# Reordering the opening of a fused attention and feed-forward kernel: exponentials, fillers, pieces and a split normalization

## The chip, the cores and the metric

The kernel runs on one core of one Trainium2 chip. The metric is the time of one execution in microseconds of the device (us), as a median of several runs. The profile is one such execution, recorded; it counts from the first instruction and its span is some 2 us shorter than the timed run. PE is the matrix engine, DVE the vector engine, ACT the scalar engine, POOL the GpSimd engine; "landing" is the time at which a load from memory is complete. Every engine's own stream is in a fixed order (the program is scheduled by hand), so an instruction that waits holds up all that stand behind it on its engine.

## The reference

```python
def _attn_ref(q, k, v):                      # each (8, 8, 576, 64): batch, heads, tokens, head size
    q_s = np.exp(q - q.max(-1, keepdims=True)); q_s /= q_s.sum(-1, keepdims=True) + 1e-09
    k_s = np.exp(k - k.max(2, keepdims=True));  k_s /= k_s.sum(2, keepdims=True) + 1e-09
    kv = np.einsum('bhsd,bhse->bhde', k_s, v)
    return np.einsum('bhsd,bhde->bhse', q_s, kv)

def _moe_ref(x, w1, w2, w3, w_out):          # x (4608, 512), d_ff 1024
    h = (x @ w1) * (x @ w2) @ w3
    return h @ w_out
```

The output of the attention, with heads and head size joined, is `x`. All inputs and the output are float32.

## The kernel before

The kernel folds `w3 @ w_out` into one matrix once ("W3O", eight groups `ft` of 128 rows): each W3 tile is loaded, cast to 16 bit, transposed on PE (`w3_t`), copied by DVE, and multiplied with `w_out` (eight matmuls for each group). Then, for each chunk of 512 tokens, `s1` makes (x @ w1) * (x @ w2) and `s2` multiplies by W3O. The attention of a batch is made of pieces: exponentials of q and k on ACT (`exp_q`, `exp_k`), sums and reciprocal on DVE (`sum_q`), a multiplication that normalizes q (`norm_q`), PE transposes of the result and a DVE copy of them (`piece_t`), `piece_kv`, and `piece_x`, which makes x. All of W3, w_out, the first batch and the w1 and w2 quarters are loaded through one queue, in that order; "fillers" are matmuls on zeros.

```python
    filler(16)
    w3_both(0)                      # cast on POOL and ACT, then w3_t
    wo_c(0, pcopy, acopy)
    filler(4)
    w3_part((0, 0))                 # (ft, gp): two of the eight matmuls of group ft
    # ... fillers 3, 3, 3 between groups 1 to 2 ...
    w3_part((2, 0), (2, 1), (0, 2), (1, 2), (2, 2))
    w3_both(3)
    wo_c(3, pcopy, acopy)
    w3_c(4, pcopy)
    w3_t(4)
    w3_part((3, 0), (3, 1), (3, 2))
    # ... last part of groups 0 to 3, each followed by its copy on ACT; w3_c(5 to 7), w3_t(5) ...
    w3_rest(4, pAB(), acopy)        # eight matmuls, then the copy into W3O
    w3_t(6)
    for hh in range(2):
        exp_q(0, 0, hh)
        sum_q(0, 0, hh)
    norm_q(0, 0, nc.gpsimd)
    w3_rest(5, pAB(), acopy)
    w3_t(7)
    # ... the same for q1, then exp_k(0, 0), v0 casts ...
    w3_rest(6, pAB(), acopy)
    piece_t(0, 0)
    wp7 = pO()
    w3_mm(wp7, 7, range(N_FT))
    piece_kv(0, (0,))
    piece_t(0, 1)
    # ... exp_k(0, 1), copy of W3O[7], v1 casts: the second qsT copy of piece_t is ahead of them on DVE ...
    piece_x(0, 0, acopy, acopy, apart=True)
    piece_kv(0, (1,), by_head=True)
    # ... piece_x(0, 1), then s1 of chunk 0 ...
```

The softmax here doesn't subtract the row's maximum and nothing guards it: scores larger than these inputs give would overflow.

## Time and profile before

| what | value |
|---|---|
| median of the first three runs | 240.61 us |
| span of the profiled run | 238.1 us |
| PE busy | 229.4 us (96%) |
| first s1 matmul of chunk 0 | 33.78 us |
| first s2 matmul of chunk 0 | 47.60 us |
| first s1 matmul of chunk 1 | 58.15 us |

The page of the kernel before: busy time of each engine with its share of the span and its instructions, then the chain of work that ended last, by engine.

```profile
PE 229.4 (96%) x1769; PEld 107.5 (45%) x1769; DVE 126.4 (53%) x214; ACT 101.3 (43%) x182; POOL 66.6 (28%) x61
...
PE 91%; DVE 5%; POOL 1%; ACT 1%; issue 1%; DVEq 0%; ACTq 0%; POOLq 0%
```

No load is in that chain. The waits of PE in the kernel before (engine, line and tile, who ended the wait: total us, how often, longest; the wait of 1.2 us at the very start is left out):

```profile
PE att L176 <- POOL eqn L138: 0.9, 1, 0.9
PE att L176 <- DVE eqn L138: 0.8, 1, 0.8
PE po L186 <- DVE kv_556 L164: 0.6, 1, 0.6
PE att L154 <- DVE v_0_73 L124: 0.5, 1, 0.5
PE po L329 <- DVE qsT L324: 0.3, 1, 0.3
```

All of them lie before 53 us; afterwards PE has no wait worth naming. The first, third and fourth belong to the first batch, the second to the second batch, the fifth to the W3 groups. The chain of waits of the kernel before from 22 to 32 us (start us, duration us, what) shows how the first batch hangs together:

```profile
22.44 0.59 ACT W3O_91 L372
23.03 0.59 ACT eq L119
...
23.64 1.43 DVE ds L131 x2
...
25.51 2.13 POOL eqn L138
27.64 0.05 issue
27.68 0.68 PE att L176 x9
28.36 1.73 PE po L329 x8
...
31.14 0.76 DVE qsT L178
31.90 0.40 DVE v_0_73 L124
```

Two facts stand out. The exponential of q0 runs behind a W3O copy at 22.44 us, though q0 landed at 20.25 us. And the last cast of v1, which landed at 29.07 us, runs only behind the second qsT copy.

The timeline of PE in the kernel before, around the fifth W3 transposes (start us, duration us, what; the idle time before it and who ended it stand in brackets).

```profile
15.64 0.61 PE L319 MATMUL att<-ident,w_288 128*128 128x128 f16 x8
16.14 0.62 PE L319 MATMUL att<-ident,w_304 128*128 128x128 f16 x8
17.04 0.60 PE L329 MATMUL po<-wo_83,qsT 128*128 128x512 f16 x2 [0.28 <-DVE qsT L324]
```

The trace says that the fifth transposes (w_304) were released at 16.09 us by POOL's cast of that tile; the last fillers had ended at 13.34 us.

### The profile page before, as it was taken

Reading aid. Unit: us, or ns where it says so; the run is one execution under the profiler, and the core shown is the slowest. Engines: PE = TensorE matmul, PEld = TensorE weight load, DVE = VectorE, ACT = ScalarE, POOL = GpSimd, SP = SyncE. Lnnn points to the kernel's source line nnn. Section 1 sums busy time; section 2 is a strip of 40 time slices with the busy share of each in tenths; the row PEclk is TensorE's granted clock in tenths of the full one; section 3 lists DMA queues with packets and bytes.
Section 4 is the critical chain, followed back from the end, with each engine's and each line's share of the span. In section 5 each row is a group of like instructions: output and inputs, shape, how many; then the busy total and the mean of one; then the engine's idle time right before and its main releaser. Section 6 shows DMA issues by size and latency. Waiting matters only on the chain.

```text
span 238.1 us, 4550 instructions
## 1 busy us (share of the span) xinstructions
PE 229.4 (96%) x1769; PEld 107.5 (45%) x1769; DVE 126.4 (53%) x214; ACT 101.3 (43%) x182; POOL 66.6 (28%) x61
## 2 busy tenths in 40 slices
PE   8999889989999999999999999999999999999993
PEld 2455444444444444444444444444444444444442
DVE  0232854498847745854763586477464344343432
ACT  4425953664665644643545354346441112222100
POOL 3453776080370260361045036023400000000000
PEclk9999999999999999999999999999999999999999
DMA  6999999999269999659979929932632222232244
GB/s 248 395 408 390 373 349 364 391 392 365 63 129 383 391 278 331 256 110 303 376 154 340 377 46 247 322 107 47 122 70 44 44 44 47 46 70 60 45 91 132
DMA packets 39702, 52.08 MB, mean 219 GB/s; under 512 B 16512, under 2 KB 20864, under 8 KB 39680
## 3 DMA queue, kind: packets, MB, share of 16 engines
q1 hardware_dynamic: 39280, 51.26, 69.2%
q10 hardware_dynamic: 400, 0.52, 0.8%
q8 instruction: 14, 0.23, 0.4%
q14 instruction: 8, 0.07, 0.1%
HBM read 38.80 MB, written 9.44 MB: 203 GB/s over the span
## 4 chain that ended last, share of the span: by engine, by line
PE 91%; DVE 5%; POOL 1%; ACT 1%; issue 1%; DVEq 0%; ACTq 0%; POOLq 0%
PE pab L239 52%; PE po L286 20%; PE pab L286 5%; PE att L377 3%; PE pab L329 3%; PE att L154 3%; PE att L186 2%; PE po L329 2%; DVE ds L131 1%; PE att L319 1%; POOL eqn L138 1%; DVE qsT L324 1%; PE att L176 1%; DVE eqn L138 1%; ACT eq L119 1%
## 5 line engine op out<-in xcount | busy, mean ns | idle before, releaser
L138 POOL TENSOR_TENSOR eqn<-eq,dr 128x1152 f16<-128x1152 f16 x15 | 31.7, 2116 | 89.6 <-DVE dr L136 59.5
L286 PEld LDWEIGHTS <-abT 128*128 128x128 f16 x296 | 28.4, 98 | 32.7 <-DVE abT L249 0.4
L288 DVE TENSOR_SCALAR osb<-po 128x512 f32<-128x512 f32 (+1 forms) x29 | 19.8, 683 | 22.1 <-PE po L286 19.1
L131 DVE TENSOR_REDUCE ds<-eq 128x9 f32<-128x576 f16 x32 | 23.6, 746 | 1.1 <-ACT eq L119 1.1
L119 ACT ACTIVATE eq<-st 128x576 f16<-128x576 f32 x32 | 21.2, 689 | 0.3 <-DMA st<-in_q_dram 0.3
L112 ACT ACTIVATE ek<-st 128x576 f16<-128x576 f32 x32 | 20.7, 682 | 0.0
L239 PE MATMUL pab<-xT,w_0_75 128*128 128x512 f16 x72 | 18.5, 379 | 0.0
L239 PE MATMUL pab<-xT,w_3_78 128*128 128x512 f16 x72 | 18.4, 380 | 0.0
L239 PE MATMUL pab<-xT,w_2_77 128*128 128x512 f16 x72 | 18.4, 380 | 0.0
L239 PE MATMUL pab<-xT,w_1_76 128*128 128x512 f16 x72 | 18.3, 379 | 0.0
L239 PE MATMUL pab<-xT,w_1_80 128*128 128x512 f16 x72 | 18.3, 379 | 0.0
L239 PE MATMUL pab<-xT,w_2_81 128*128 128x512 f16 x72 | 18.3, 379 | 0.0
L239 PE MATMUL pab<-xT,w_3_82 128*128 128x512 f16 x72 | 18.3, 379 | 0.0
L239 PE MATMUL pab<-xT,w_0_79 128*128 128x512 f16 x72 | 18.3, 379 | 0.0
L202 ACT CAST xT<-att 128x512 f16<-128x512 f32 x14 | 7.5, 589 | 10.6 <-PE att L186 10.6
L239 PEld LDWEIGHTS <-w_0_79 128*128 128x128 f16 x72 | 7.0, 98 | 8.8 <-issue 0.6
L286 PE MATMUL po<-W3O_87,abT 128*128 128x512 f16 (+1 forms) x29 | 10.9, 377 | 0.0
L286 PE MATMUL po<-W3O_88,abT 128*128 128x512 f16 (+1 forms) x29 | 10.9, 376 | 0.0
L286 PE MATMUL po<-W3O_89,abT 128*128 128x512 f16 (+1 forms) x29 | 10.9, 376 | 0.0
L286 PE MATMUL po<-W3O_90,abT 128*128 128x512 f16 (+1 forms) x29 | 10.9, 376 | 0.0
L286 PE MATMUL po<-W3O_91,abT 128*128 128x512 f16 (+1 forms) x29 | 10.9, 376 | 0.0
L286 PE MATMUL po<-W3O_92,abT 128*128 128x512 f16 (+1 forms) x29 | 10.9, 376 | 0.0
(315 smaller groups left out, 352.6 us busy)
## 6 DMA issues: line engine op xcount, KB each, us to landing
st<-in_q_dram SPq DMA_DIRECT2D x16, 576.0 KB, 8.7
st<-in_k_dram SPq DMA_DIRECT2D x16, 576.0 KB, 7.1
st<-in_v_dram SPq DMA_DIRECT2D x15, 576.0 KB, 7.8
out_dram<-osb SPq DMA_DIRECT2D x67, 128.0 KB, 2.6
st<-in_moe_w_dram SPq DMA_DIRECT2D x15, 512.0 KB, 9.0
st<-in_moe_w_out_dram SPq DMA_DIRECT2D x4, 512.0 KB, 7.0
st<-in_v_dram SPq DMA_DIRECT2D x2, 288.0 KB, 11.8
st<-in_moe_w_dram SPq DMA_DIRECT2D x2, 256.0 KB, 10.7
```

Of the source, the lines that this page charges most:

```text
L112: nc.scalar.activation(out=eks[(b, i)][:, :, hh, :], in_=qkv32[("k", b, i)][:, hh].rearrange("p (r d) -> p r d", r=R), func=AF.Exp)
L119: nc.scalar.activation(out=eqs[(b, i)][:, :, hh, :], in_=qkv32[("q", b, i)][:, hh].rearrange("p (r d) -> p r d", r=R), func=AF.Exp)
L131: nc.vector.tensor_reduce(out=dss[(b, i)][:, :, hh], in_=eqs[(b, i)][:, :, hh, :], axis=AX.X, op=ALU.add)
L138: eng.tensor_tensor(out=eqn.rearrange("p r h d -> p (r h) d"), in0=eqs[(b, i)].rearrange("p r h d -> p (r h) d"), in1=dr[:, :, None].broad ...
L154: nc.tensor.matmul(kvp[64 * hh:64 * hh + 64, g, 65 * i:65 * i + 65], lhsT=eks[(b, i)][rows, r, hh], rhs=v16buf[b % 2][rows, 2 * i + hh, r, ...
L186: nc.tensor.matmul(out.rearrange("p (r s) -> p r s", s=SP), lhsT=kvs[(b, i)][rows, g], rhs=qsTs[(b, i)][rows, r0:r1, 64 * g:64 * g + 64], ...
L202: copy(out=dst[:, hh], in_=xps[hh])
L239: nc.tensor.matmul(p, lhsT=wsb[qt][:, ct, fo:fo + P], rhs=xT[:, ct, t0:t0 + CH], start=(ct == 0), stop=(ct == N_CT - 1))
L286: nc.tensor.matmul(po[:, 0:n1 - n0], lhsT=abT[(j, ft)][:, tb * P:(tb + 1) * P], rhs=W3O[ft][:, n0:n1], start=(ft == 0), stop=(ft == N_FT - 1))
L288: nc.vector.tensor_scalar(out=osb[:, n0:n1], in0=po[:, 0:n1 - n0], scalar1=ISC, scalar2=None, op0=ALU.mult)
L329: nc.tensor.matmul(wps, lhsT=w3Ts[ft][:, gt, :], rhs=wosb[gt // 2][:, gt % 2, :], start=(gt == 0), stop=(gt == N_FT - 1))
L377: nc.tensor.matmul(wp[:, 0], lhsT=zero[:, 0:P], rhs=zero, start=True, stop=True)
```

## The change

The intent: put the q exponentials of the first batch ahead of the W3O copies on ACT, cut fillers from 29 matmuls to 16, put pieces of the first batch between the last W3O groups, and split each normalization of the second batch over DVE and POOL. Two things are not in the cut below: the cast of the first w1 quarter is all on POOL (a quarter of it was on ACT), and the casts of v of the second batch stand elsewhere in the order. The diff, cut to its core:

```diff
-    filler(16)
+    filler(8)
     w3_both(0)
     wo_c(0, pcopy, acopy)
-    filler(4)
+    filler(2)
     # ... three more filler(3) become filler(2) ...
-    w3_part((2, 0), (2, 1), (0, 2), (1, 2), (2, 2))
+    w3_part((2, 0), (2, 1), (0, 2))
     w3_both(3)
+    w3_part((1, 2), (2, 2))
     wo_c(3, pcopy, acopy)
-    w3_c(4, pcopy)
+    w3_c(4, pcopy, acopy)
+    w3_part((3, 0), (3, 1), (3, 2))
     w3_t(4)
-    w3_part((3, 0), (3, 1), (3, 2))
     # ...
-    w3_rest(4, pAB(), acopy)
+    w3_mm(wps[4], 4, range(N_FT))
     w3_t(6)
+    for i in range(2):
+        for hh in range(2):
+            exp_q(0, i, hh)
+            sum_q(0, i, hh)
+        norm_q(0, i, nc.gpsimd)
+        if i == 0:
+            acopy(out=W3O[4], in_=wps[4])
+            w3_mm(wps[5], 5, range(N_FT))
+            w3_t(7)
     # ... exp_k(0, 0), v0 casts, copy of W3O[5] ...
+    w3_mm(wps[6], 6, range(N_FT))
+    w3_mm(wps[7], 7, range(4))
     piece_t(0, 0)
-    wp7 = pO()
-    w3_mm(wp7, 7, range(N_FT))
-    piece_kv(0, (0,))
-    piece_t(0, 1)
+    w3_mm(wps[7], 7, range(4, N_FT))
     # ... exp_k(0, 1), copies of W3O[6], W3O[7] ...
+    piece_kv(0, (0,))
     # ... v1 casts, now ahead of the second qsT copy ...
+    piece_t(0, 1)
-    piece_x(0, 0, acopy, acopy, apart=True)
+    piece_x(0, 0, acopy, acopy, apart=(pAB, pAB))
     # ... second batch:
-    norm_q(1, 0, nc.gpsimd)        # within s1 of the last pair
-    norm_q(1, 1, nc.vector)
+    norm_q(1, 0, nc.vector, nc.gpsimd)   # behind that pair; rows 0:5 on DVE, 5:9 on POOL
+    norm_q(1, 1, nc.vector, nc.gpsimd)
-    s2(0, 0, alt=True)
+    s2(0, 0, alt=True, on_act=True)      # result scaled and copied by ACT, also for s2(0, 1)
     piece_t(1, 0)
-    piece_t(1, 1)
     s2(0, 2, alt=True)
+    piece_t(1, 1)
```

More of the change, by code (lines that the diff above doesn't have):

```diff
@@ L132, in sum_q, with norm_q @@
                                 axis=AX.X, op=ALU.add)
-    def norm_q(b, i, eng):
-        dr = drs[(b, i)].rearrange("p r h -> p (r h)")
-        nc.vector.reciprocal(out=dr, in_=dss[(b, i)].rearrange("p r h -> p (r h)"))
+    def norm_q(b, i, *engs):
+        dr = drs[(b, i)]
+        nc.vector.reciprocal(out=dr.rearrange("p r h -> p (r h)"),
+                             in_=dss[(b, i)].rearrange("p r h -> p (r h)"))
         eqn = attn.tile([P, R, 2, D], F16, tag="eqn", name="eqn", bufs=4)
-        eng.tensor_tensor(
-            out=eqn.rearrange("p r h d -> p (r h) d"),
-            in0=eqs[(b, i)].rearrange("p r h d -> p (r h) d"),
-            in1=dr[:, :, None].broadcast_to([P, 2 * R, D]), op=ALU.mult)
+        cuts = (0, R) if len(engs) == 1 else (0, 5, R)
+        for eng, r0, r1 in zip(engs, cuts, cuts[1:]):
+            eng.tensor_tensor(
+                out=eqn[:, r0:r1].rearrange("p r h d -> p (r h) d"),
+                in0=eqs[(b, i)][:, r0:r1].rearrange("p r h d -> p (r h) d"),
+                in1=dr[:, r0:r1].rearrange("p r h -> p (r h)")[:, :, None].broadcast_to(
+                    [P, 2 * (r1 - r0), D]), op=ALU.mult)
         eqns[(b, i)] = eqn
@@ L188, in x_mm, with piece_x @@
                          start=True, stop=True)
-    def piece_x(b, i, *copies, apart=False):
+    def piece_x(b, i, *copies, apart=()):
         if apart:
-            xps = [pO(), pAB()]
+            xps = [p() for p in apart]
         else:
@@ L277, with s2 @@
     outv = out.rearrange("(b s r) c -> b r s c", r=R, s=SP)
-    def s2(j, tb, alt=False, cuts=(0, C), mid=None):
+    def s2(j, tb, alt=False, cuts=(0, C), mid=None, on_act=False):
         osb = ffn.tile([P, C], F32, tag="osb", name="osb", bufs=4)
@@ L287, in s2 @@
                                  rhs=W3O[ft][:, n0:n1], start=(ft == 0), stop=(ft == N_FT - 1))
-            nc.vector.tensor_scalar(out=osb[:, n0:n1], in0=po[:, 0:n1 - n0], scalar1=ISC,
-                                    scalar2=None, op0=ALU.mult)
+            if on_act:
+                nc.scalar.mul(out=osb[:, n0:n1], in_=po[:, 0:n1 - n0], mul=ISC)
+            else:
+                nc.vector.tensor_scalar(out=osb[:, n0:n1], in0=po[:, 0:n1 - n0], scalar1=ISC,
+                                        scalar2=None, op0=ALU.mult)
             for h in range(2):
@@ L368, in w3_part @@
             w3_mm(wps[ft], ft, (2 * gp, 2 * gp + 1))
-    def w3_rest(ft, wp, copy):
-        w3_mm(wp, ft, range(N_FT))
-        copy(out=W3O[ft], in_=wp)
     def filler(n):
@@ L377, in filler @@
             nc.tensor.matmul(wp[:, 0], lhsT=zero[:, 0:P], rhs=zero, start=True, stop=True)
-    filler(16)
+    filler(8)
     w3_both(0)
     wo_c(0, pcopy, acopy)
-    filler(4)
+    filler(2)
     w3_part((0, 0))
-    filler(3)
+    filler(2)
     w3_both(1)
     wo_c(1, pcopy, acopy)
-    filler(3)
+    filler(2)
     w3_part((1, 0), (0, 1), (1, 1))
@@ L390 @@
     wo_c(2, pcopy, acopy)
-    filler(3)
-    w3_part((2, 0), (2, 1), (0, 2), (1, 2), (2, 2))
+    filler(2)
+    w3_part((2, 0), (2, 1), (0, 2))
     w3_both(3)
+    w3_part((1, 2), (2, 2))
     wo_c(3, pcopy, acopy)
-    w3_c(4, pcopy)
+    w3_c(4, pcopy, acopy)
+    w3_part((3, 0), (3, 1), (3, 2))
     w3_t(4)
-    w3_part((3, 0), (3, 1), (3, 2))
     for ft in range(4):
@@ L404 @@
     w3_c(7, pcopy)
-    w3_rest(4, pAB(), acopy)
+    wps += [pAB(), pAB(), pAB(), pO()]
+    w3_mm(wps[4], 4, range(N_FT))
     w3_t(6)
-    for hh in range(2):
-        exp_q(0, 0, hh)
-        sum_q(0, 0, hh)
-    norm_q(0, 0, nc.gpsimd)
-    w3_rest(5, pAB(), acopy)
-    w3_t(7)
-    for hh in range(2):
-        exp_q(0, 1, hh)
-        sum_q(0, 1, hh)
-    norm_q(0, 1, nc.gpsimd)
+    for i in range(2):
[7 more added lines that the diff above has]
+            w3_t(7)
     exp_k(0, 0, 0)
@@ L421 @@
     cast_v(0, 0, acopy, slice(1, 2))
-    w3_rest(6, pAB(), acopy)
+    acopy(out=W3O[5], in_=wps[5])
+    w3_mm(wps[6], 6, range(N_FT))
+    w3_mm(wps[7], 7, range(4))
     piece_t(0, 0)
-    wp7 = pO()
-    w3_mm(wp7, 7, range(N_FT))
-    piece_kv(0, (0,))
-    piece_t(0, 1)
+    w3_mm(wps[7], 7, range(4, N_FT))
     exp_k(0, 1, 0)
     exp_k(0, 1, 1)
-    acopy(out=W3O[7], in_=wp7)
+    acopy(out=W3O[6], in_=wps[6])
+    acopy(out=W3O[7], in_=wps[7])
+    piece_kv(0, (0,))
     cast_v(0, 1, pcopy, slice(0, 1))
@@ L433 @@
     cast_v(0, 1, pcopy, slice(1, 2), slice(5, 9))
-    piece_x(0, 0, acopy, acopy, apart=True)
+    piece_t(0, 1)
+    piece_x(0, 0, acopy, acopy, apart=(pAB, pAB))
     piece_kv(0, (1,), by_head=True)
-    cast_w(0, 0, acopy, slice(0, 2), slice(0, P))
-    cast_w(0, 0, pcopy, slice(0, 2), slice(P, 2 * P))
-    cast_w(0, 0, pcopy, slice(2, 4), slice(0, P))
-    cast_w(0, 0, pcopy, slice(2, 4), slice(P, 2 * P))
+    for cts in (slice(0, 2), slice(2, 4)):
+        for f in range(2):
+            cast_w(0, 0, pcopy, cts, slice(f * P, f * P + P))
     x8 = pAtt([P, 2, 512], F32)
     x8_mm(0, [x8[:, 0], x8[:, 1]], (0,))
-    piece_x(0, 1, acopy, vcopy, apart=True)
+    piece_x(0, 1, acopy, vcopy, apart=(pAB, pO))
     x8_mm(0, [x8[:, 0], x8[:, 1]], (1,))
@@ L459 @@
     sum_q(1, 0, 0)
-    def second_q():
-        exp_q(1, 0, 1)
-        sum_q(1, 0, 1)
-        norm_q(1, 0, nc.gpsimd)
-    s1_pair(0, (6, 7), second_q, lambda: (exp_q(1, 1, 0), exp_q(1, 1, 1)))
+    s1_pair(0, (6, 7), lambda: exp_q(1, 0, 1), lambda: (exp_q(1, 1, 0), exp_q(1, 1, 1)))
+    sum_q(1, 0, 1)
+    norm_q(1, 0, nc.vector, nc.gpsimd)
     sum_q(1, 1, 0)
     sum_q(1, 1, 1)
-    norm_q(1, 1, nc.vector)
+    cast_v(1, 0, pcopy)
+    norm_q(1, 1, nc.vector, nc.gpsimd)
     exp_k(1, 0, 0)
     exp_k(1, 0, 1)
-    cast_v(1, 0, pcopy)
-    s2(0, 0, alt=True)
+    s2(0, 0, alt=True, on_act=True)
     exp_k(1, 1, 0)
     exp_k(1, 1, 1)
-    s2(0, 1)
-    piece_t(1, 0)
-    piece_t(1, 1)
     cast_v(1, 1, pcopy, slice(0, 1))
     cast_v(1, 1, acopy, slice(1, 2))
+    s2(0, 1, on_act=True)
+    piece_t(1, 0)
     pc = pieces(1)
     s2(0, 2, alt=True)
+    piece_t(1, 1)
     pc[0]()
```

## The prediction

> What bounds it now. The page gives a span of 238.1 us, PE busy 229.4 us (96%); the chain of waits is 91% PE. From 58.2 us, where chunk 1 starts, the timeline of PE shows no gap worth naming, so the change can pay only in its first 58 us. There the page's DMA row is at 9 tenths: load landings are fixed by the queue (last W3 tile 18.75, q0 20.25, q1 23.02, last half of v1 29.07, w2 first quarter 32.07, last half batch-1 v 50.20 us).
>
> Three losses in that stretch. (1) By the timelines, the first-batch q exps wait for the W3O_91 copy (22.44), itself behind PE, although q0 landed at 20.25; sum, reciprocal and POOL normalization (2.12 us) follow, and the first-batch transposes wait 0.93 us on PE (27.68). (2) The last v1 cast, landed 29.07, sits on DVE behind the second qsT copy, runs at 31.82; PE then waits 0.55 us, and 0.56 us for kv. s1 starts at 33.78. (3) Second-batch transposes wait 0.83 us for DVE's eqn (52.62).
>
> What the change does. It removes 13 fillers (8 initial, 5 at 216 ns each): PE reaches the fourth W3 transposes when its cast is ready (about 13.1, was 15.64), so W3O groups end 2 us earlier. q exps start at about 20.3, POOL's first eqn is ready near 24.9 (was 27.63). The v1 cast runs at once (29.1); first-batch kv, x follow the landing: s1 starts at about 31.4, gain 2.3 us. It cannot start much earlier: w2's first quarter is cast by 32.7 and needed 1.73 us after s1's start. Later quarters are cast at 34.67 to 42.23, each 0.2 to 1.5 us before need.
>
> Second batch: landings again bound it. The split costs less than it seems: the Trainium skill (SBUF — State Buffer, section "Who interferes with whom") says a DVE instruction with two SBUF inputs excludes a GpSimd instruction that reads SBUF. This trace agrees: POOL's v cast took 1.80 us beside DVE's eqn, 0.66 elsewhere. So the halves run one after the other, estimated 0.7 + 0.95 us, hardly better than one engine. I estimate eqn(1,0) at 48.8, eqn(1,1) at 51.5, last v cast 52.2, kv about 52.3 (was 54.95), chunk 1's s1 at 55.5 (was 58.15). Moving two evictions to ACT (0.6 us each) costs nothing there.
>
> Sum: 2.3 us from the first batch, about 0.3 more from the second: 2.6 us, all kept by the PE-bound rest. Predicted 238.0 us, range 236.8 to 239.6. Chances: faster by over 2% 0.03, within 0.94, slower 0.03.
>
> What would show it. Timelines: first filler ends about 4.8, w_3 transposes at 13.1; first eqn ends about 24.9; first s1 matmul 31.0 to 31.9; chunk-0 s2 about 45.3; POOL's eqn half stretched beyond 0.95 us or DVE's beyond 0.7; chunk 1's s1 near 55.5; from there every later instruction shifted by the same 2.6 us. Landing times unchanged to 0.3 us.
>
> What would make it wrong. The fillers keep the clock: the Trainium skill (TensorE: Matmul & The Clock Gate, section "What's actually happening") has half rate until a busy window of some 3.4 us; in this trace full clock begins 5.8 us in, and the removed 8 leave gaps under 1 us, so I expect it to stay. If not, PE falls behind the loads and up to 2 us go. Second: w1/w2 quarters landing late, with POOL casts just in time, could stall s1. Third: the eqn halves colliding with POOL's v cast longer than I assume, which would take the second-batch 0.3 us and more. On the other side, if q1 lands earlier and both batches run at landing times, the gain is 3.5 us.

## The result, and the profile after

The changed kernel took 237.94 us (median of 4 runs, 237.59 to 238.45), the kernel before 240.75 us (median of 4, 240.04 to 241.52). The ratio is 0.9884, with a 95% interval of 0.9849 to 0.992: a gain of 1.2%.

The page of the changed kernel, same parts:

```profile
PE 227.0 (96%) x1756; PEld 106.3 (45%) x1756; DVE 125.6 (53%) x213; ACT 102.8 (44%) x184; POOL 66.9 (28%) x63
...
PE 76%; DMA 18%; SPq 2%; POOL 1%; ACT 1%; issue 0%; DVE 0%
```

PE lost 2.4 us of busy time, the 13 fillers, and the span fell by 2.3 us. That looks like a full explanation; the experiments show that it is a coincidence. The second line seems to be a better clue: loads (DMA) now hold 18% of the chain. Between 24 and 53 us the chain of waits of the changed kernel reads:

```profile
17.31 10.98 DMA st<-in_v_dram
28.29 8.96 DMA st<-in_moe_w_dram
...
37.30 0.94 POOL w L93
38.24 11.03 DMA st<-in_k_dram
...
49.29 1.27 ACT ek L112 x2
...
50.58 1.63 POOL eqn L141
...
52.25 0.40 PE att L180 x4
```

This clue fails, though. The loads are on the path to a k load of the second batch, not on that to the start of s1, and they enter the chain only by the step from ACT's exponential of k (until 50.56 us) to POOL's half of a normalization (from 50.58 us). The program has no such dependency: that exponential stands behind the normalization, which does not read its result. In the run with the old fillers (below) the same exponential ended at 50.31 us and the same multiplication began only at 50.81. In both profiles it begins as POOL's cast of v ahead of it ends (50.62 and 50.85 us). The view infers its links from the times of semaphores, and here it took a coincidence for a cause. Whether loads bind has to be read from the timelines and tested.

The timeline of PE in the changed kernel, from the first batch's transposes to s1:

```profile
26.52 0.68 PE L180 MATMUL att<-ident,eqn 128*128 128x128 f16 x9
27.03 1.03 PE L336 MATMUL po<-wo,eqn 128*128 128x512 f16 x4
27.99 0.48 PE L158 MATMUL att<-v,ek 64*64 64x65 f16 x36
28.71 0.68 PE L180 MATMUL att<-ident,eqn 128*128 128x128 f16 x9 [0.24 <-DVE rc L166]
...
30.97 0.22 PE L190 MATMUL att<-qsT,kv 64*64 64x64 f16 x4 [0.19 <-DVE qsT L182]
31.37 0.40 PE L190 MATMUL pab<-qsT,kv 64*64 64x512 f16 x1 [0.18 <-DVE kv L168]
```

and DVE's in the same stretch, which answers to the end of the chain shown of before:

```profile
29.76 0.49 DVE L124 CAST v<-st 128x320 f16<-128x320 f32 x1 [0.73 <-DMA st<-in_v_dram]
30.16 0.75 DVE L182 COPY qsT<-att 128x1152 f16<-128x1152 f16 x1
```

The v1 cast stood idle for its load and ran 0.02 us after the landing at 29.74 us; in the kernel before it ran 2.75 us after the landing (31.82 against 29.07). The three waits of the first batch, 2.0 us together, became three of 0.2 us each.

| landmark, us | before | after | predicted |
|---|---|---|---|
| last half of v1 landed | 29.07 | 29.74 | unchanged |
| first s1 matmul of chunk 0 | 33.78 | 31.74 | 31.4 |
| first s2 matmul of chunk 0 | 47.60 | 45.78 | 45.3 |
| second-batch kv | 54.95 | 52.58 | 52.3 |
| first s1 matmul of chunk 1 | 58.15 | 55.88 | 55.5 |

The loads landed 0.6 to 1.1 us later in this profile than in that of before. This is no effect of the change: the second W3 tile landed at 6.99 us in the profile of before, at 8.05 in that of after, and between 7.1 and 8.4 in every other profile in which its record is there. Measured from the landing of v1, s1 came 4.71 us later before and 2.00 us later after.

This distance is the better clue. It is 2.00 or 2.01 us in the changed kernel and in three of the experiments on it below (second-batch part undone, exponentials behind, one more load), while the landing itself moves from 29.45 to 31.02 us. So in these four s1 follows the load. In the other runs it is 2.65 to 5.56 us, but for the try at a better version, which moves the first s1 matmuls themselves. Within s1 loads cost the changed kernel another 0.2 us: the second w1 quarter landed at 34.26 us, POOL cast it, and PE's weight load (PEld) waited for the cast:

```profile
34.31 1.04 POOL L93 CAST w<-st 128x1024 f16<-128x1024 f32 x1 [0.62 <-DMA st<-in_moe_w_dram]
```

```profile
35.40 0.55 PEld L243 LDWEIGHTS <-w 128*128 128x128 f16 x4 [0.53 <-POOL w L93]
```

The matmul behind it began 0.42 us after the one before, where 0.22 is usual. The kernel before has no such step.

### The profile page after: what moved, and what is told of

Read it like the earlier page. It is cut to its first block, busy times and chain, and to the rows that moved or that the text cites. A ratio compares the mean times of both kernels' runs of the same rounds, so it can differ in the third digit from the quotient of the medians. Undisturbed runs are those within 1.5% of the kernel's fastest.

```text
span 235.8 us, 4526 instructions
## 1 busy us (share of the span) xinstructions
PE 227.0 (96%) x1756; PEld 106.3 (45%) x1756; DVE 125.6 (53%) x213; ACT 102.8 (44%) x184; POOL 66.9 (28%) x63
## 4 chain that ended last, share of the span: by engine, by line
PE 76%; DMA 18%; SPq 2%; POOL 1%; ACT 1%; issue 0%; DVE 0%
PE pab L243 48%; PE po L290 20%; DMA st<-in_moe_w_dram 9%; DMA st<-in_k_dram 5%; DMA st<-in_v_dram 5%; PE pab L290 4%; PE att L158 2%; PE att L190 2%; SPq L103 1%; SPq L97 1%; POOL eqn L141 1%; ACT ek L112 1%; POOL w L93 0%; PE att L180 0%; DVE osb L295 0%
## 5 line engine op out<-in xcount | busy, mean ns | idle before, releaser
L243 PE MATMUL pab<-xT,w 128*128 128x512 f16 x576 | 130.8, 379 | 0.1
L243 PEld LDWEIGHTS <-w 128*128 128x128 f16 x576 | 55.3, 98 | 66.8 <-issue 0.9
L248 ACT CAST a<-pab 128x512 f16<-128x512 f32 x72 | 41.8, 586 | 94.9 <-PE pab L243 94.9
L253 DVE TENSOR_TENSOR abT<-pab,a 128x512 f16<-128x512 f32 x72 | 49.7, 690 | 58.7 <-PE pab L243 56.5
L141 POOL TENSOR_TENSOR eqn<-eq,dr 128x1152 f16<-128x1152 f16 (+1 forms) x16 | 32.8, 2052 | 84.7 <-DVE dr L136 49.1
L290 PE MATMUL po<-W3O,abT 128*128 128x512 f16 (+1 forms) x232 | 54.2, 376 | 0.0
L124 POOL CAST v<-st 128x1152 f16<-128x1152 f32 (+2 forms) x16 | 16.2, 1037 | 0.5 <-DMA st<-in_v_dram 0.4
L290 PE MATMUL pab<-W3O,abT 128*128 128x512 f16 (+1 forms) x64 | 14.2, 363 | 0.0
L93 POOL CAST w<-st 128x1024 f16<-128x1024 f32 (+2 forms) x11 | 8.6, 792 | 4.0 <-DMA st<-in_moe_w_dram 4.0
L208 DVE CAST xT<-att 128x1024 f16<-128x1024 f32 x7 | 8.5, 1208 | 0.8 <-PE pab L190 0.8
```

Source lines behind the costliest of these rows:

```text
L93: copy(out=(w1sb, w2sb)[wi][qt][:, cts, cols], in_=w32[(wi, qt)][:, cts, cols])
L124: copy(out=v16buf[b % 2][:, 2 * i:2 * i + 2, rs, 0:D][:, hhs], in_=qkv32[("v", b, i)].rearrange("p h (r d) -> p h r d", r=R)[:, hhs, rs])
L141: eng.tensor_tensor(out=eqn[:, r0:r1].rearrange("p r h d -> p (r h) d"), in0=eqs[(b, i)][:, r0:r1].rearrange("p r h d -> p (r h) d"), in1= ...
L243: nc.tensor.matmul(p, lhsT=wsb[qt][:, ct, fo:fo + P], rhs=xT[:, ct, t0:t0 + CH], start=(ct == 0), stop=(ct == N_CT - 1))
L248: nc.scalar.copy(out=a16, in_=pa)
L253: nc.vector.tensor_tensor(out=ab, in0=pb, in1=a16, op=ALU.mult)
```

## The experiments

Three theories were put to the test. The landing theory (that of the prediction): in the first 58 us PE waits for whatever comes last, the order of work or the loads; the change takes the order out of the way, and the loads bind. The rival "PE work": the span fell because PE had 2.4 us less to do. The rival "exponentials": the early q exponentials are what the first batch gained. Gains are given as ratio to the kernel before, and in us as 240.6 times its distance from 1.

### The parts, one by one

Only the fillers, on the kernel before:

```diff
-    filler(16)
+    filler(8)
-    filler(4)
+    filler(2)
-    filler(3)      # three times
+    filler(2)
```

> The kernel before with only the 13 fillers cut; order and second batch as before. Rival (PE work): the gain of the whole change is the 2.4 us of PE busy time that the fillers took, so this run has all of it, about -2.4 to -2.8 us. Landing theory: the first s1 matmul comes when the later of two chains is through, the PE chain or the chain from the loads; with old order the v1 cast still waits behind the second qsT copy, so s1 starts about 32.3 (was 33.78, 31.74 after), and the total falls by 1.5 to 2.0 us, clearly less than the whole change.

Measured: 240.39 us, ratio 0.9987 (0.997 to 1.0005), a gain of 0.3 us at best. PE busy fell to 227.2 us, as in the changed kernel, and nearly nothing came of it. "PE work" falls, but the landing theory's own number (1.5 to 2.0 us) missed as well. The timeline of PE in this run shows why:

```profile
14.89 0.61 PE L319 MATMUL att<-ident,w 128*128 128x128 f16 x8
17.04 0.62 PE L319 MATMUL att<-ident,w 128*128 128x128 f16 x8 [1.54 <-POOL w L307]
17.50 1.46 PE L329 MATMUL po<-wo,qsT 128*128 128x512 f16 x6
```

PE reaches the fourth transposes earlier in relation to the loads, and then stands for 1.54 us at the fifth, whose W3 tile POOL casts whole. The six matmuls of group 3, which could have run in that time, are behind it in PE's order. The fillers had only covered this wait.

All of the change, with the old fillers (16, 4, 3, 3, 3):

> The changed kernel with the old filler counts (16, 4, 3, 3, 3). Rival (PE work): none of the gain is left, within 0.4 us of before. Landing theory: the W3O groups end some 2 us later, but the new order waits for loads of q, k, v there, so PE has slack; s1 starts at 31.6 to 32.2, and at least 2.0 us of the gain stay.

Measured: 238.04 us, ratio 0.9901 (0.9876 to 0.9926), a gain of 2.4 us with PE busy at 229.6 us, as much as in the kernel before (229.4). This settles it against "PE work": the same work, 2.4 us faster. The intervals allow the fillers some tenths of a us on top. The fillers did make PE later here (the first batch's transposes at 27.54 us instead of 26.52), and s1 came 2.65 us behind the landing of v1 instead of 2.00; but chunk 1 began only 0.13 us later than in the changed kernel (56.01 against 55.88), partly as s1 no longer waited for the w1 quarter.

Only the second-batch part, on the kernel before (edit: the second-batch lines of the diff above):

> The kernel before with only the second-batch part (split norms, evictions on ACT, moved casts and transposes). Rival (PE work): no PE work is removed, 0. Landing theory: s1 starts at 33.8 as before; the 0.83 us wait of PE for the second-batch normalization goes, -0.6 to -0.9 us.

Measured: 240.03 us, ratio 0.9976 (0.9959 to 0.9993), a gain of 0.6 us. The wait of 0.83 us at the second-batch transposes shrank to 0.27 us.

All but the second-batch part (edit: those lines undone in the changed kernel):

> The changed kernel with the second-batch part as before. Both theories expect most of the gain: PE work -2.4 us; landing theory -2.3 to -2.8 us, s1 start at 31.7 and chunk 1 within 0.3 us of the changed kernel's 55.9, because the old single normalization on DVE then has its inputs earlier. What it tells: if chunk 1 starts over 0.5 us later than 55.9, the second-batch part is worth that on top.

Measured: 238.48 us, ratio 0.9917 (0.989 to 0.9943), a gain of 2.0 us. Chunk 1 began at 56.73 us, 0.85 us later than in the changed kernel, 0.21 us of which were there at the first s2 matmul already (45.99 against 45.78), as v1 had landed 0.21 us later; the old wait is back in PE's timeline:

```profile
51.21 0.68 PE L180 MATMUL att<-ident,eqn 128*128 128x128 f16 x9 [0.83 <-DVE eqn L141]
```

So the second-batch part is worth about 0.6 us here too.

Only the early q exponentials, on the kernel before:

```diff
-    w3_rest(4, pAB(), acopy)
+    w3_mm(wps[4], 4, range(N_FT))
     w3_t(6)
     # exp_q(0, 0), sum_q, norm_q
+    acopy(out=W3O[4], in_=wps[4])     # and the same for group 5
```

> The kernel before with only the first-batch q exps ahead of the W3O copies on ACT; fillers, pieces and second batch as before. If the exps are the whole of the first-batch gain (rival), s1 starts 2 us earlier and the total falls by about 2 us. Landing theory: the 0.93 us wait before the first transposes goes, but PE itself is no earlier, and the v1 cast still waits behind the second qsT copy; about -0.9 us, between -0.5 and -1.3.

Measured: 240.49 us, ratio 0.9993 (0.9975 to 1.0011): nothing. ACT's timeline, and then DVE's, of this run:

```profile
21.69 1.29 ACT L119 ACTIVATE eq<-st 128x576 f16<-128x576 f32 x2
```

```profile
23.69 0.69 DVE L324 COPY eqn<-att 128x1024 f16<-128x1024 f16 x1 [1.48 <-PE att L319]
24.30 1.40 DVE L131 TENSOR_REDUCE ds<-eq 128x9 f32<-128x576 f16 x2
```

The exponentials were done at 22.98 us, but the sums began only at 24.30: ahead of them on DVE is the copy of the seventh W3 transposes, which waits for PE. Both the prediction and the expectation followed ACT and overlooked DVE's order.

Only the new order of the last W3O groups and first-batch pieces, on the kernel before:

```diff
+    w3_mm(wp7, 7, range(4))
     piece_t(0, 0)
-    w3_mm(wp7, 7, range(N_FT))
-    piece_kv(0, (0,))
-    piece_t(0, 1)
+    w3_mm(wp7, 7, range(4, N_FT))
+    # exp_k(0, 1), W3O copies, piece_kv(0, (0,)), v1 casts, and then
+    piece_t(0, 1)
```

> The kernel before with only the new order of the last W3O groups and first-batch pieces (half a W3O group ahead of the first transposes, v1 cast ahead of the second qsT copy). If the exps are the whole of the gain (rival): 0. Landing theory: PE's 0.93 us wait is filled by half a group (4 matmuls, 0.86 us), and the v1 cast runs when it lands, so the 0.55 us wait goes too: about -1.0 us, between -0.6 and -1.5. Together with the run of exps alone it should make up most of the first-batch gain of 2.1 us.

Measured: 239.34 us, ratio 0.995 (0.9927 to 0.9973), a gain of 1.2 us. This is the largest single part. The edit holds more than its two named moves: `piece_kv` and the copy of W3O[6] stand later, x is made in other PSUM tiles, and the first w1 quarter is cast on POOL alone, as in the whole change. What each of these is worth was not tested. In the trace PE's wait of 0.93 us before the first transposes is gone, the v1 cast ran at 30.36 us, ahead of the second qsT copy (30.84), and s1 came 3.62 us behind the landing of v1 instead of 4.71.

### The parts within the changed kernel

The q exponentials behind the W3O copies again:

```diff
     w3_mm(wps[4], 4, range(N_FT))
+    acopy(out=W3O[4], in_=wps[4])
     w3_t(6)
     # and the copy of W3O[5] ahead of the exponentials of q1
```

> The changed kernel with its q exps behind the W3O copies on ACT again, all else as changed. If the early exps matter only together with the other moves: the normalization comes late, s1 starts 0.5 us or more later, total -1.5 to -2.2 us against before. If they are worth nothing (in the run of exps alone they moved 1.5 us earlier and the sums on DVE did not, for DVE runs in order and had the copy of the seventh W3 transposes first): within 0.4 us of the changed kernel, -2.4 to -2.9 us against before.

Measured: 237.81 us, ratio 0.9893 (0.9867 to 0.9919). That is a gain of 2.6 us, as much as the changed kernel's 2.8 within the noise. The move that the title names first is worth nothing that these runs can tell, alone or in company.

The old order around the fourth and fifth W3 groups:

```diff
-    w3_part((2, 0), (2, 1), (0, 2))
+    w3_part((2, 0), (2, 1), (0, 2), (1, 2), (2, 2))
     w3_both(3)
-    w3_part((1, 2), (2, 2))
     wo_c(3, pcopy, acopy)
-    w3_c(4, pcopy, acopy)
-    w3_part((3, 0), (3, 1), (3, 2))
+    w3_c(4, pcopy)
     w3_t(4)
+    w3_part((3, 0), (3, 1), (3, 2))
```

> The changed kernel with the old order around the fourth and fifth W3 groups (the cast of the fifth W3 tile whole on POOL, six matmuls of group 3 behind the fifth transposes), all else as changed. If this move is what brings PE ahead (in the run of fillers alone PE stood 1.5 us at the fifth transposes, waiting for that cast): W3 matmuls end 1.2 to 1.5 us later, s1 starts about 0.8 us later, total -1.6 to -2.2 us against before. If the landing of v1 sets s1 alone: no loss, -2.4 to -2.9 us.

Measured: 238.52 us, ratio 0.993 (0.9908 to 0.9952), a gain of 1.7 us, so 0.9 us less than the run before it in the same rounds (2.6 us); the two intervals overlap a little, so the size is rough. The wait of 1.5 us at the fifth transposes is back, and s1 starts at 32.68 us after a landing of v1 at 29.19: 3.49 us behind it instead of 2.00. So it was this move that brought the earlier PE which the prediction put down to the fillers. Its two halves (order of matmuls, cast on two engines) were not tested apart.

### Is it the loads that bind?

One more load of 512 KB, which nothing reads, ahead of the first q load, in both kernels:

```diff
+    extra = konst.tile([P, Fd], F32, name="extra")
+    nc.sync.dma_start(out=extra, in_=moe_w3[0:P, :])
     for which, i in LOADS:
```

> The kernel before with one more load of 512 KB (never read) ahead of the first q load; every later landing comes about 1.3 us later. Landing theory: in the kernel before, PE and the order of work are what s1 waits for, its casts run 0.7 to 2.7 us after their landing, so 0 to +0.5 us. If the kernel before is bound by loads as well, +1.3 us.

> The changed kernel with the same additional load. Landing theory: the first batch now follows its landings (the last v1 half, w1 and w2 quarters), so the whole delay comes through: +1.0 to +1.4 us against the changed kernel, about -1.6 us against before. Rival (PE work): PE does the same work, so no change: -2.6 us against before.

Measured: on the kernel before 240.47 us, ratio 0.9992 (0.9972 to 1.0011), no cost. On the changed kernel 239.19 us, ratio 0.9942 (0.9917 to 0.9966): of its gain of 2.8 us 1.4 are left, so the load cost 1.4 us. Its interval and that of the changed kernel just overlap, so the size is rough, but the traces agree: the last half of v1 landed 1.28 us later in both kernels (30.35 against 29.07 us, 31.02 against 29.74), and s1 moved by 0.27 us in the kernel before (33.78 to 34.05) and by 1.28 us in the changed one (31.74 to 33.02). The delay is free before and paid after; PE does the same work in both. With the constant 2.00 us behind the landing this shows that the change moved the first batch from "bound by order" to "bound by loads". The sums on DVE now wait for q ahead of a W3 copy, and PE waited 1.03 us for that copy; but s1 stood no further behind v1's landing, so this wait was not what set it.

### No fillers at all

```diff
-    filler(8)      # and all other fillers of the changed kernel
```

> The changed kernel with no fillers at all. If fillers only fill idle time and the clock warms from the work itself: full clock comes some 3 to 7 us later in the records, PE makes up the delay while it waits for loads, within 0.6 us of the changed kernel. If they are needed for the clock: half rate well into the W3 groups, PE behind the loads at the first transposes, +1 us or more against the changed kernel.

Measured: 240.75 us, ratio 1.0002 (0.9967 to 1.0037): the whole gain is gone. The trace's first clock record grants full clock from 19.2 us on, against 5.0 us in the changed kernel. It holds no record of the time before, so the page's row of the clock shows no difference; that the clock was lower until then is read from the matmuls. Two matmuls of the same form on PE in this run, then in the changed kernel:

```profile
6.72 1.03 PE L336 MATMUL pab<-wo,qsT 128*128 128x512 f16 x2 [0.79 <-DVE qsT L331]
```

```profile
6.50 0.59 PE L336 MATMUL pab<-wo,qsT 128*128 128x512 f16 x2 [0.64 <-POOL wo L320]
```

PE cannot make up for that while it waits for loads: the first transposes came at 30.68 us instead of 26.52, and s1 at 35.33. Two of the six runs took 239.1 us and four 240.7 to 241.6, so the moment at which the clock rises seems to vary; only one run has a trace, so this stays open. Fillers are thus worth little as such (13 of 29 could go for 0.3 to 0.4 us) and 2.7 us or so as what brings the clock up early.

### A try at a better version

```diff
+    pas01 = [pAB(), pAB()]
+    for fb in range(2):
+        s1_mm(pas01[fb], w1sb, 0, fb, range(2))   # first four s1 matmuls
     x8_mm(0, [x8[:, 0], x8[:, 1]], (0,))
-    piece_x(0, 1, acopy, vcopy, apart=(pAB, pO))
+    piece_x(0, 1, acopy, vcopy)
     # w1 and w2 second quarters: half of the cast on ACT
-    norm_q(1, 0, nc.vector, nc.gpsimd)
-    norm_q(1, 1, nc.vector, nc.gpsimd)
+    norm_q(1, 0, nc.gpsimd)                        # in the last s1 pair, as before
+    norm_q(1, 1, nc.vector)
```

> A try at a better version: the changed kernel with the first four s1 matmuls ahead of the last first-batch piece, the second w1 and w2 quarters cast on two engines, and the second-batch normalizations whole again, one on POOL, one on DVE. Landing theory: s1 starts 0.4 to 0.7 us earlier after the same landing of v1, the 0.27 us wait at the last second-batch transposes goes; 0.5 to 0.9 us faster than the changed kernel, -3.2 to -3.7 us against before. If the quarters of w1 and w2 bound it already: no better than the changed kernel.

Measured: 238.39 us, ratio 0.9918 (0.9896 to 0.9941): a gain of 2.0 us, no better than the changed kernel. PE's timeline, and then DVE's, of this run:

```profile
31.03 1.28 PE L243 MATMUL pab<-xT,w 128*128 128x512 f16 x4 [0.23 <-POOL w L93]
32.24 0.47 PE L190 MATMUL att<-qsT,kv 64*64 64x64 f16 x12
33.37 0.38 PE L243 MATMUL pab<-xT,w 128*128 128x512 f16 x1 [0.66 <-ACT xT L206]
34.09 2.10 PE L243 MATMUL pab<-xT,w 128*128 128x512 f16 x9 [0.35 <-DVE xT L206]
```

```profile
33.35 0.69 DVE L206 CAST xT<-att 128x512 f16<-128x512 f32 x1 [2.01 <-ACT xT L206]
```

s1 did start 0.7 us earlier (31.03). But the matmuls put first held up the piece whose result the rest of s1 waits for (its group of matmuls began at 32.24 us; in the changed kernel the piece's began at 31.37). That piece now writes one PSUM tile, and its two copies ran one after the other (the trace has DVE's wait for ACT's; that the shared tile is the reason was not tested). Chunk 0's s2 came 1.05 us later (46.83 against 45.78). The second-batch half of the edit did work: from there to chunk 1 it took 9.53 us instead of 10.10. The changed kernel with that half alone was not run; that it would gain 0.5 us is an estimate from this one profile.

## Why the prediction was right or wrong

The number was right (238.0 us predicted, 237.94 measured), and so was its frame: s1 follows the landing of the last v1 half, and all later work keeps the shift. That the number came out to a tenth of a us is partly luck: two of the moves that it counted on gained next to nothing, and two terms that it had too small or under another name made up for them. Point by point:

- **The v1 cast behind the second qsT copy (right).** It ran 0.02 us after its landing instead of 2.75, and the new order of pieces alone gained 1.2 us.
- **"It removes 13 fillers ... so W3O groups end 2 us earlier" (wrong cause).** Fillers alone gained 0.3 us or nothing. Without them PE stood 1.54 us at the fifth W3 tile, whose cast was not ready; the fillers had hidden that. Moving six matmuls of group 3 ahead of that wait, and halving the cast, was worth 0.9 us. The prediction's sum came out although this term stood under the wrong name.
- **"q exps start at about 20.3, POOL's first eqn is ready near 24.9" (wrong).** The exponentials did start as q0 landed (21.32 us after a landing at 21.30), but the first normalization was done only at about 26.5 us, 5.2 us behind that landing where the prediction has 4.65. The sums on DVE stand behind the copy of the seventh W3 transposes. The early exponentials were worth nothing in both directions. It did not cost the sum, as half a W3O group now fills PE until then.
- **Halves of a normalization run one after the other (right).** POOL's and DVE's timelines of the changed kernel:

```profile
47.94 1.59 POOL L141 TENSOR_TENSOR eqn<-eq,dr 128x512 f16<-128x512 f16 x1 [5.11 <-ACT ek L112]
```

```profile
47.80 0.82 DVE L141 TENSOR_TENSOR eqn<-eq,dr 128x640 f16<-128x640 f16 x1
```

  POOL's half took 1.59 us where 0.94 is its share of the 2.12 us for the whole (an estimate: 512 of 1152 columns); it began beside DVE's and ended 0.91 us after DVE's had ended at 48.62. This agrees with the Trainium skill, SBUF — State Buffer, section "Who interferes with whom". Split, it took 1.7 us from the start on DVE to the end on POOL, against 2.1 on POOL alone. The second normalization gained nothing by the split: it took 1.85 us from DVE's start at 50.35 to POOL's end at 52.20, against 1.72 whole on DVE before.
- **The second batch worth 0.3 us (a term too small).** It measured 0.6 us alone, and about as much within the whole. The kernel before's 0.83 us wait shrank to 0.27, for another block of s2 (1.7 us of matmuls) now stands ahead of the last transposes.
- **Landing times unchanged to 0.3 us (wrong, without effect on the reasoning).** The last half of v1 landed between 28.96 and 29.95 us in the profiles without the additional load, which is why the landmarks after are 0.3 to 0.5 us later than predicted.
- **w1 and w2 quarters could stall s1 (right, at 0.2 us).** It is the step at 35.40 us shown above.
- **The clock stays up with fewer fillers (right),** with full clock from 5.0 us on. With none, full clock comes only at 19.2 us.

By single removals and additions, the gain of 2.8 us (1.9 to 3.6 by its interval) is made up of the new order of the pieces (1.2 us), the order around the fifth W3 group (0.9 us) and the second batch (0.6 us); fillers and exponentials share what is left, about 0.1 us, which is less than the intervals can tell. The parts need not add up: the first two come from additions to the kernel before and removals from the changed one, and an earlier s1 meets loads that bind again.

## What to carry to other kernels

An engine that is busy with fillers need not be the bottleneck: follow the real instructions and ask what released each, before counting removed fillers as a gain. When an instruction is moved earlier on one engine, check the in-order queue of the next engine in the chain for what stands ahead of its consumer, or the move is worth nothing. To learn whether a stage is bound by loads, delay the loads: an unread load that costs nothing in one kernel and its full time in the other tells it in two runs. And before a chain of waits is believed, check in the program that its links are dependencies.

## What the Trainium skill lacked or had wrong

- TensorE: Matmul & The Clock Gate, section "What's actually happening", gives full clock after one busy window of about 3.4 us, but no figure for how much waiting inside it is too much. Without fillers PE was busy for 4.2 of the 7 us from 5 to 12 us and 6.2 of the next 7, with waits of 0.8 to 1.2 us, and full clock came only at 19.2 us, after PE had been busy without a wait from 15.16 us on. Once up, the clock held through waits of up to the same length (0.64, 1.25 and 0.35 us between 5.8 and 10.2 us in the changed kernel, busy for 4.75 of the 7 us from 5 to 12 us). These are one profile each.
- No page that was looked up tells how much the landing of loads varies from run to run in a stretch where the DMA engines are busy for 9 tenths and more: the second W3 tile landed between 6.99 and 8.42 us in the profiles, the last half of v1 between 28.96 and 29.95.
- SBUF — State Buffer, section "Who interferes with whom", was right here: 1.59 us instead of an estimated 0.94 us for POOL beside a DVE multiplication with two SBUF inputs.
